# Top-1 routing moved into the attention stage, a fixed 448 places per expert, and expert weights in attention's buffers

## The chip, the cores and the metric

The kernel runs on one core of a Trainium2 chip: TensorE (PE, with its weight loads PEld), VectorE (DVE), ScalarE (ACT), GpSimd (POOL) and SyncE (SP), which run at their own pace and wait for one another by semaphores, and 16 DMA engines that move data between the chip's main memory and the on-chip buffers. The metric is the device time of one execution in microseconds, the median of several runs.

## What is computed

A gated linear attention, followed by a mixture of experts in which every token goes to one expert. The reference, cut to what matters:

```python
# 4 batches, 8 heads, 768 positions, 48 wide; complex state S
for t in range(S):
    S_re, S_im = a_re*S_re - a_im*S_im + k_t v_t^T, a_re*S_im + a_im*S_re
    y[t] = q_t @ S_re                       # a is first limited to |a| <= 0.999
x = y as 3072 rows of 384
logits = x @ w_gate                         # 8 experts
expert_idx = argmax(logits)
gate_w = softmax(logits)[expert_idx]
for e in range(8):
    mask = expert_idx == e
    h = max(x[mask] @ w1[e], 0)             # 384 -> 1024
    out[mask] = gate_w[mask] * (h @ w2[e])  # 1024 -> 384
```

All is fp32. How many tokens an expert gets depends on the data.

## The kernel before

**Attention** (lines 200 to 556) works batch by batch. Per batch, VectorE and ScalarE limit the gates (`limit`), run the recurrence over blocks of 16 positions (`front`, `fix`), and fold q and k with it (`fold`); SyncE's DMAs turn the folded tiles `pk` into one slot per head (`QX`, `KX`, a ring of six). Then `attention(b, g)` goes over the six chunks of 128 positions for a group of heads (three groups a batch): TensorE forms scores, VectorE masks them (`am`), TensorE forms outputs and the carried state (`st`, copied by ScalarE), ScalarE evicts rows to `xf`. In the last group of a batch each chunk's rows of `xf` are turned by TensorE, copied (`xt`) and multiplied by the routing weights `wgate` into logits; a SyncE DMA takes the rows to a table `x_hbm` in main memory, and the logits of a batch are copied to `lg_all`. None of this is emitted in the order of the source: each operation is registered with an engine, a cost, a delay and what it waits for, and a planner (`in_time`, lines 81 to 120) simulates them in turn, with priorities, and emits them in the order of their planned starts. The order on an engine is then fixed. In the profile they all carry line 132, where `InOrder` issues them.

**General path** (lines 559 to 637): `good` collects whether the numbers stayed in range. From it two trip counts are computed (`trips`, line 570), 0 or the whole count, of two loops: a slow exact recurrence and its logits. Every engine loads the counts and branches over the loops if they are 0.

**Routing** (lines 640 to 774), for all 3072 tokens at once: softmax gate, one-hot of the maximum, ranks within an expert by products with a triangular matrix (`rk`, lines 706 and 707), prefix sums, and an inversion by one-hot products (`A`, `J`, `ids`, line 757) which gives the lists `idx` (token of each place) and `widx` (weight rows of each tile). Experts are rounded up to whole tiles of 128 tokens; 31 tiles are always enough.

**Experts** (lines 777 to 815): 31 tiles in turn. GpSimd gathers the 128 token rows (`xs`, line 785) and the whole weights of the tile's expert (`w1t`, `w2t`, 3.1 MB, triple buffered); TensorE transposes the rows (`xt_ps`, line 797), multiplies 24 blocks of `w1t` (`h_ps`, line 804), ScalarE and VectorE apply the maximum with 0 (`ht`), TensorE multiplies by `w2t` (`o_ps`, line 810), VectorE multiplies by the gate (`yo`, line 812) and GpSimd scatters the rows to the output (line 813).

Of the kernel before, what the change touches and what calls it, by code (L numbers as in the profile page):

```python
# [33 lines left out]
W = DM + 1  # L34
LEAST = 1e-20
# [100 lines left out]
def gateloop_then_moe(ctx, tc, q, k, a_re, a_im, v, wg, w1, w2, out):  # L136
    nc = tc.nc
    x_hbm = nc.dram_tensor("x_hbm", (N + 1, W), FP32, kind="Internal").ap()

# [20 lines left out]
    with tc.tile_pool(name="zero", bufs=1) as setup:  # L160
        zrow = setup.tile([1, W], FP32, name="zrow")
        nc.vector.memset(zrow, 0.0)
        nc.sync.dma_start(x_hbm[N:N + 1, :], zrow)

# [30 lines left out]
    lg_all = route.tile([128, NT, E], FP32, name="lg_all")  # L195
    good = route.tile([128, B, G * C + 4], FP32, name="good")

    with ExitStack() as att:
# [13 lines left out]


# [9 lines left out]
        gates = [buf(f"gate{i}", JQ, 3, NC) for i in range(BL // JQ)]  # L223
        X = buf("X", BL, 2, NC)
        last, carry, zc = buf("last", 3, NC), buf("carry", 2, G * C, NB), [buf(f"zc{i}", 2, 2, G * C) for i in range(2)]
        lim = [[buf(f"{n}{i}", JQ, NC) for n in ("ls", "ll", "lu")] for i in range(2)]
        lsq, fsq = buf("lsq", JQ, 2, NC), buf("fsq", BL, 2, C * NB)
        fx = [buf(f"fx{i}", BL * C * (NB - 1)) for i in range(4)]
        zs = [buf(f"z{i}", 2, 2, NC) for i in range(2)]
# [4 lines left out]
        xf = buf("xf", C, DM)  # L234
# [6 lines left out]
        lg_ps = ps[7][:, 0:C * E].rearrange("p (c e) -> p c e", e=E)  # L241

        ops, used = [], {}
# [14 lines left out]
        def dma(late, emit, after=(), free=()):  # L258
            return op("S", 0.62, late, emit, after, free)

# [45 lines left out]
        def front(b, tiles):  # L306
# [5 lines left out]
            o = None  # L312
            for j in range(1, BL):
# [9 lines left out]
                state["z", w] = [o]  # L323
                state.setdefault(("gate", j // JQ), []).extend([m, c0] if j == 1 else [m])
# [19 lines left out]
            for t in tiles:  # L344
                state["carried", t] = [o, c0]
                state["X", t], state["carry", t] = [], []

# [74 lines left out]
        def attention(b, g):  # L422
# [24 lines left out]
            for c in range(C):  # L447
# [37 lines left out]
                def gather(c=c):  # L485
                    if own[0] == own[n - 1]:
                        A.activation(xf[:, c, hs[0] * D:hs[-1] * D + D].rearrange("p (h e) -> p h e", e=D), y_ps[:, 0:n, own[0]],
                                     func=ACT.Copy, scale=-1.0)
                    else:
                        for i, h in enumerate(hs):  # L490
                            A.activation(xf[:, c, h * D:h * D + D], y_ps[:, i, own[i]], func=ACT.Copy, scale=-1.0)
# [27 lines left out]
                if g == G - 1:  # L519
                    rows = state["row", b, c]  # L520

                    def across(c=c):
                        for d in range(DT):
                            T.transpose(px_ps[:, d, :], xf[:, c, d * 128:d * 128 + 128], ident)
# [9 lines left out]
                    r0 = b * S + c * 128  # L534
                    away = dma(5.0, lambda c=c, r0=r0: Q.dma_start(x_hbm[r0:r0 + 128, 0:DM].rearrange("(n j) w -> j n w", j=BL), xf[:, c, :]), rows)
                    state["xf", c] = [away, px]
            for i in slots:
                state["head", i] = [y]
            if g == G - 1:
                copy = act(C * E, lambda: A.copy(lg_all[:, b * C:(b + 1) * C, :], lg_ps), [lg], first=1)  # L540
                state["lg"] = [copy]
# [3 lines left out]
        for b in range(B):  # L545
            front(b, range(G))
            fixed = [fix(t) for t in range(G)]
            for t in range(G):
                fold(b, t, fixed[t])
                attention(b, t)  # L550
            if b + 1 < B:
                load_gates(b + 1)
                limit(b + 1)
        for o in in_time(ops):
            o.emit()


    with ExitStack() as fs:
        fp = fs.enter_context(tc.tile_pool(name="fp", bufs=1))
        fps = fs.enter_context(tc.tile_pool(name="fps", bufs=1, space=PSUM))  # L560
        nc.vector.tensor_scalar(out=good[:, :, G * C:], in0=good[:, :, G * C:], scalar1=MOST, scalar2=None, op0=ALU.is_le)
        least = fp.tile([128, 1], FP32, name="least")
        nc.vector.tensor_reduce(least, good.rearrange("p n c -> p (n c)"), axis=AX, op=ALU.min)
        ones_f = fp.tile([128, 1], FP32, name="ones_f")
        nc.vector.memset(ones_f, 1.0)
        n_good = fps.tile([1, 1], FP32, name="n_good")
        nc.tensor.matmul(n_good, lhsT=least, rhs=ones_f, start=True, stop=True)
        trips = fp.tile([1, 2], I32, name="trips")
        for u, n in enumerate((S // BL, NT)):
            nc.vector.tensor_scalar(out=trips[:, u:u + 1], in0=n_good, scalar1=127.5, scalar2=float(n),  # L570
                                    op0=ALU.is_lt, op1=ALU.mult)
        BG = B * G
        state = fp.tile([128, 2, BG, D], FP32, name="state")
        nc.gpsimd.memset(state, 0.0)  # L574

        own_i = fp.tile([128, G, H], I32, name="own_i")
        nc.gpsimd.iota(own_i, pattern=[[128, G], [-D, H]], base=0, channel_multiplier=1)
        own_f = fp.tile([128, G, H], FP32, name="own_f")
        nc.vector.tensor_copy(own_f, own_i)
        own = fp.tile([128, G, H], FP32, name="own")  # L580
        nc.vector.tensor_scalar(out=own, in0=own_f, scalar1=0.0, scalar2=None, op0=ALU.is_ge)
# [275 lines left out]
```

## Time and profile before

| | |
|---|---|
| time, median of 3 runs | 768.36 us (765.04 to 769.07) |
| profiled run | 768.0 us, span from first to last instruction 766.3 us |
| mean granted clock of TensorE | 0.946 |
| busy: PE, PEld, DVE, ACT, POOL | 79%, 68%, 51%, 37%, 18% |
| DMA | 156.50 MB, of which 108.36 MB on GpSimd's queue |

The page gives the busy time of each engine over the whole span and in 40 slices; a busy share over the span mixes the stages. The stretches give the same for chosen windows. The lines in order of time give the start, the length, the engine, source line and tiles of instructions or of runs of equal ones (x48), and in brackets how long the engine had been idle and what ended the idling. A record of a matrix product is one pass; an fp32 product makes two.

### The profile page before, as it was taken

Reading aid. Unit: us, or ns where it says so; the run is one execution under the profiler, and the core shown is the slowest. Engines: PE = TensorE matmul, PEld = TensorE weight load, DVE = VectorE, ACT = ScalarE, POOL = GpSimd, SP = SyncE. Lnnn points to the kernel's source line nnn. Section 1 sums busy time; section 2 is a strip of 40 time slices with the busy share of each in tenths; the row PEclk is TensorE's granted clock in tenths of the full one; section 3 lists DMA queues with packets and bytes.
Section 4 is the critical chain, followed back from the end, with each engine's and each line's share of the span. In section 5 each row is a group of like instructions: output and inputs, shape, how many; then the busy total and the mean of one; then the engine's idle time right before and its main releaser. Section 6 shows DMA issues by size and latency. Waiting matters only on the chain. (4 is left out here: it accounts for less than half of the span.)

```text
span 766.3 us, 11061 instructions
## 1 busy us (share of the span) xinstructions
PE 602.1 (79%) x3985; PEld 521.7 (68%) x3985; DVE 387.1 (51%) x720; ACT 280.3 (37%) x870; POOL 137.8 (18%) x160
## 2 busy tenths in 40 slices
PE   0000499789973999899317999999999999999997
PEld 0000499789963998899306787787787777787775
DVE  3999999989999999741261111111111111111111
ACT  4653799579985866775200000000000000000000
POOL 8000000000000000000112332342332442343221
PEclk9999999779985999999757999999999999999999
DMA  7131883486528706721019779789778988778930
GB/s 223 40 88 25 200 211 102 109 208 172 147 70 192 182 25 167 194 73 43 25 27 413 291 287 349 279 331 383 267 308 332 360 322 338 294 290 338 338 127 1
DMA packets 67630, 156.50 MB, mean 204 GB/s; under 512 B 9873, under 2 KB 50866, under 8 KB 59634
## 3 DMA queue, kind: packets, MB, share of 16 engines
q0 software_dynamic: 12896, 108.36, 36.9%
q1 hardware_dynamic: 51474, 47.36, 23.9%
q8 instruction: 33, 0.54, 0.3%
q10 hardware_dynamic: 3200, 0.01, 0.2%
q14 instruction: 27, 0.22, 0.1%
HBM read 127.23 MB, written 10.83 MB: 180 GB/s over the span
## 5 line engine op out<-in xcount | busy, mean ns | idle before, releaser
L804 PEld LDWEIGHTS h_ps<-xt,w1t 128*128 128x128 f32 x1488 | 172.9, 194 | 13.0 <-issue 5.0
L804 PE MATMUL h_ps<-xt,w1t 128*128 128x128 f32 x1488 | 173.2, 277 | 4.7 <-issue 4.7
L810 PE MATMUL o_ps<-w2t,ht 128*128 128x384 f32 x496 | 167.8, 492 | 8.5 <-ACT ht L806 8.2
L132 PE MATMUL bank<-QX,KX 128*128 128x224 f32 (+1 forms) x384 | 87.4, 367 | 102.6 <-DVE fl L132 86.1
L806 ACT ACTIVATE ht<-h_ps 128x512 f32<-128x512 f32 x31 | 18.5, 597 | 356.3 <-PE h_ps L804 356.3
L132 PEld LDWEIGHTS bank<-QX,KX 128*128 128x128 f32 x384 | 70.4, 207 | 105.0 <-issue 86.0
L810 PEld LDWEIGHTS o_ps<-w2t,ht 128*128 128x128 f32 x496 | 91.7, 190 | 71.7 <-ACT ht L806 14.2
L132 PE MATMUL bank<-st,QX 128*128 128x128 f32 x576 | 109.9, 279 | 1.7 <-ACT st L132 1.7
L812 DVE TENSOR_SCALAR yo<-o_ps,xs 128x384 f32<-128x384 f32 x31 | 19.2, 618 | 143.4 <-PE o_ps L810 143.4
L132 PEld LDWEIGHTS bank<-st,QX 128*128 128x128 f32 x576 | 87.9, 195 | 2.9 <-ACT st L132 2.9
L799 DVE COPY xt<-xt_ps 128x384 f32<-128x384 f32 x31 | 17.2, 556 | 139.4 <-PE xt_ps L797 139.4
L132 ACT ACTIVATE QX<-diag,KX 96x48 f32<-96x48 f32 x320 | 80.6, 329 | 3.8 <-DMA KX<-pk 3.7
L132 PE MATMUL bank<-vb,am 128*128 128x128 f32 x384 | 73.5, 282 | 4.9 <-DVE am L132 3.0
L813 POOL DMA_INDIRECT out_dram<-yo,idx x31 | 31.5, 1016 | 194.0 <-DVE yo L812 193.1
L132 PEld LDWEIGHTS bank<-vb,am 128*128 128x128 f32 x384 | 60.3, 196 | 6.6 <-DVE am L132 3.7
L574 POOL MEMSET state<- 128x1152 f32 x1 | 1.1, 1062 | 353.6 <-DMA x_hbm<-xf 353.6
L132 DVE TENSOR_TENSOR am<-bank,causal 128x256 f32<-128x256 f32 x120 | 43.0, 363 | 33.8 <-PE bank L132 28.9
L132 PE MATMUL bank<-vb,kt 128*128 128x128 f32 x320 | 59.4, 278 | 0.2 <-ACT kt L132 0.2
L132 PEld LDWEIGHTS bank<-vb,kt 128*128 128x128 f32 x320 | 48.2, 195 | 0.3 <-issue 0.3
L132 DVE TENSOR_TENSOR z<-gate,X 128x576 f32<-128x576 f32 x56 | 42.0, 750 | 0.6
L132 DVE TENSOR_TENSOR fx<-X,carry 128x672 f32<-128x672 f32 x48 | 38.5, 848 | 0.0
L785 POOL DMA_INDIRECT xs<-x_hbm,idx x31 | 30.2, 975 | 26.0 <-DVE idx L765 16.9
(143 smaller groups left out, 658.5 us busy)
## 6 DMA issues: line engine op xcount, KB each, us to landing
KX<-pk SPq DMA_DIRECT2D x48, 146.2 KB, 4.1
QX<-pk SPq DMA_DIRECT2D x48, 144.0 KB, 3.7
gate<-in_a_re_dram SPq DMA_DIRECT2D x16, 288.0 KB, 3.1
gate<-in_a_im_dram SPq DMA_DIRECT2D x16, 288.0 KB, 3.5
qt<-in_q_dram SPq DMA_DIRECT2D x12, 384.0 KB, 4.7
kt_in<-in_k_dram SPq DMA_DIRECT2D x12, 384.0 KB, 5.6
vb<-in_v_dram SPq DMA_DIRECT2D x24, 192.0 KB, 3.6
x_hbm<-xf SPq DMA_DIRECT2D x24, 192.0 KB, 2.9
```

The costliest lines, as they stand in the source:

```text
L132: return lambda *a, **kw: self.tc.keep_in_program_order(f(*a, **kw))
L574: nc.gpsimd.memset(state, 0.0)
L785: nc.gpsimd.indirect_dma_start(out=o, out_offset=None, in_=src, in_offset=bass.IndirectOffsetOnAxis(ap=index, axis=0))
L799: nc.vector.tensor_copy(xt, xt_ps)
L804: nc.tensor.matmul(h_ps[:, f, :], lhsT=w1t[:, c:c + 128], rhs=xt[:, d, :], start=(d == 0), stop=(d == DT - 1))
L806: nc.scalar.activation(ht[:, 0:FT // 2, :], h_ps[:, 0:FT // 2, :], func=ACT.Relu)
L810: nc.tensor.matmul(o_ps, lhsT=ht[:, f, :], rhs=w2t[:, f * DM:f * DM + DM], start=(f == 0), stop=(f == FT - 1))
L812: nc.vector.tensor_scalar_mul(y, o_ps, xs[:, DM:W])
L813: nc.gpsimd.indirect_dma_start(out=out[:, :], out_offset=bass.IndirectOffsetOnAxis(ap=idx[:, j:j + 1], axis=0), in_=y, in_offset=None, bou ...
```

## The change

Routing is done while attention runs, in five sends: one for each of the first three batches, and two for the last (chunks 0 to 3, chunks 4 and 5). A send computes the gate, the one-hot and the rank of each token within its expert, adds the next free row of the expert (`free_row`, carried from send to send), and scatters the rows from `xf` (now one buffer per chunk, 386 wide, with the gate and the token's number in the last two columns) straight to their place in a sorted table `sorted_x`. An expert has 448 places there that are used; they are filled beforehand with rows whose token number is out of range, so that their outputs are dropped. `x_hbm` is no longer written in attention.

The experts are then eight blocks of 448 places with plain loads of rows and weights: three tiles of 128 outputs and one half tile of 64. For the half tile the 384 output columns are split in two products of 192 that write to partitions 0 to 63 and 64 to 127 of one bank. Weights of three experts are held in `big[0..2]`; attention's gates, limits and squares, and X with its products, live in slices of the same buffers, and the first three fetches are planned on SyncE as soon as these are read for the last time.

The general path, now with the old routing and the old experts inside it, sits ahead of the experts in one loop of 0 or 1 trips. It runs if a number was out of range or an expert has more than 448 tokens; the experts then run after it on blank rows.

The diff, cut to its core:

```diff
+sends = [(b, 0, C) for b in range(B - 1)] + [(B - 1, 0, 4), (B - 1, 4, C)]
+big = [keep.tile([128, n], FP32, name=f"big{i}") for i, n in enumerate((12 * BL * NC // 4, 7296, 7296))]
+def fetch(e, queue):
+    for w, at, n in ((w1, 0, DT * F), (w2, DT * F, FT * DM)):
+        queue.dma_start(big[e % 3][:, at:at + n], w[e * 128:e * 128 + 128])
-gates = [buf(f"gate{i}", JQ, 3, NC) for i in range(BL // JQ)]
-X = buf("X", BL, 2, NC)
+gates = [part(0, JQ, 3, NC) for i in range(BL // JQ)]
+X = part(2, BL, 2, NC)
...
 lg = pe(3, logits, [turned_x], state.get("lg", []), first=rank)
-away = dma(5.0, lambda c=c, r0=r0: Q.dma_start(x_hbm[r0:r0 + 128, 0:DM].rearrange("(n j) w -> j n w", j=BL), xf[:, c, :]), rows)
-state["xf", c] = [away, px]
+for n_send, (sb, c0, c1) in enumerate(sends):
+    if (sb, c1 - 1) == (b, c):
+        send(n_send, b, c0, c1 - c0, lg)
...
+def send(k, b, c0, n, lg):
+    o = dve(wide, lambda: V.tensor_reduce(top, logit, axis=AX, op=ALU.max), [lg], free)
+    d = dve(wide, lambda: vtt(sub, logit, bc(top[:, :, None], full), ALU.subtract), [o])
...
+    T.matmul(rank, lhsT=before, rhs=oh, start=True, stop=(n == 1))
...
+    for i in range(n):
+        m = act(2, lambda i=i: A.copy(xfs[c0 + i][:, DM:WS], mark[:, i, :]), [gate, number], state.get(("xf", c0 + i), []))
+        move = pool_dma(4.0, away, [s, m, *state["blank"]] + state["row", b, c0 + i])
+        state["xf", c0 + i] = [move, state["x row", c0 + i]]
...
+for e in range(3):
+    op("S", 1.3, 20.0, lambda e=e: fetch(e, Q), (), wait)
...
+xs = load(0, room())
...
+stt(fine[:, 2:3], fine[:, 1:2], float(CAP), fine[:, 0:1], ALU.is_le, ALU.mult)
+n_gen = nc.values_load(trips[0:1, 0:1], min_val=0, max_val=1, ...)
+with tc.For_i(0, n_gen, 1):
+    general()
+    load(0, xs)
-for j in range(NTILE):
-    gather(xs, x_hbm[:, :], idx[:, j:j + 1])
-    gather(w1t, w1[:, :], widx[:, j:j + 1])
-    gather(w2t, w2[:, :], widx[:, j:j + 1])
...
+xt = turned(xs)
+for e in range(E):
+    if e + 1 < E:
+        xs_next = load(e + 1, room())
+    w1t, w2t = weights(e)
+    for f in range(FT):
+        for d in range(DT):
+            T.matmul(h, lhsT=w1t[:, d, f * 128:f * 128 + 128], rhs=xt[:, d, :], start=(d == 0), stop=(d == DT - 1))
...
+    if e + 1 < E:
+        xt = turned(xs_next)
+    for i in range(TT):
+        for f in range(FT):
+            T.matmul(o, lhsT=ht[:, f, i * 128:i * 128 + 128], rhs=w2t[:, f, :], start=(f == 0), stop=(f == FT - 1))
...
+    for f in range(FT):
+        for u in range(2):
+            T.matmul(o[u * 64:u * 64 + 64, 0:HALF], lhsT=ht[:, f, TT * 128:CAP], rhs=w2t[:, f, u * HALF:u * HALF + HALF],
+                     start=(f == 0), stop=(f == FT - 1))
...
+    if e + 3 < E:
+        fetch(e + 3, nc.sync)
```

## Prediction

> **What bounds the kernel now.** I read the page's busy shares over the span first, then the stretches of the span, then the lines in order of time around the joint between the two halves, then one expert tile near the end. The page:
>
> ```profile
> span 766.3 us, 11061 instructions
> ...
> PE 602.1 (79%) x3985; PEld 521.7 (68%) x3985; DVE 387.1 (51%) x720; ACT 280.3 (37%) x870; POOL 137.8 (18%) x160
> ...
> PE   0000499789973999899317999999999999999997
> ...
> PEclk9999999779985999999757999999999999999999
> ```
>
> No engine is at 100%, so there are stages with different limits. The stretches (columns: length, then busy us of PE, PEld, DVE, ACT, POOL, then clock, DMA share, GB/s):
>
> ```profile
> 20.00:80.00 60.00, 0.00 (x0) 0.00 (x0) 59.38 (x96) 31.54 (x53) 0.00 (x0) 1.00 0.23 63
> ...
> 240.00:330.00 90.00, 83.22 (x609) 80.12 (x610) 81.97 (x150) 68.36 (x256) 0.00 (x0) 0.94 0.57 143
> ...
> 330.00:360.00 30.00, 30.00 (x242) 29.86 (x241) 8.56 (x20) 19.11 (x80) 0.00 (x0) 1.00 0.21 53
> ...
> 371.30:406.70 35.40, 2.94 (x31) 2.19 (x32) 16.82 (x63) 1.84 (x3) 9.02 (x15) 0.53 0.24 70
> ...
> 406.70:750.00 343.30, 334.48 (x2011) 264.65 (x2012) 52.69 (x89) 17.91 (x30) 111.42 (x115) 0.99 0.81 310
> ```
>
> Attention (to 371.3 us) is VectorE's until about 330 and TensorE's from there. 371 to 407 is a hole in which TensorE works 2.9 of 35.4 us. From 407 TensorE works 97%. In order of time, the joint:
>
> ```profile
> 370.45 0.83 PE L132 MATMUL bank<-wgate,xt 128*128 128x8 f32 x6 [0.57 <-ACT xt L132]
> ...
> 373.55 0.21 DVE L570 TENSOR_SCALAR trips<-n_good 1x1 int32<-1x1 f32 x2 [0.33 <-PE n_good L567]
> ...
> 379.89 0.35 DVE L683 TENSOR_REDUCE mx<-lg_all 128x24 f32<-128x192 f32 x1 [5.27 <-SPq L637]
> ...
> 397.76 1.13 POOL L785 DMA_INDIRECT xs<-x_hbm,idx  x1 [16.91 <-DVE idx L765]
> ...
> 399.19 0.95 POOL L785 DMA_INDIRECT w1t<-in_moe_w_dram,widx  x1 [0.30 <-issue]
> ...
> 406.71 7.54 PE L804 MATMUL h_ps<-xt,w1t 128*128 128x128 f32 x48 [4.65 <-issue]
> ```
>
> The last logits end at 371.3, the two skipped loops cost 373.8 to 379.8, routing on VectorE 379.9 to 397.5, the first rows and weights 397.8 to 406.7. Then one tile of the experts:
>
> ```profile
> 738.52 5.52 PE L804 MATMUL h_ps<-xt,w1t 128*128 128x128 f32 x48
> ...
> 743.88 0.49 PE L797 MATMUL xt_ps<-ident,xs 128*128 128x128 f32 x3
> ...
> 744.73 5.43 PE L810 MATMUL o_ps<-w2t,ht 128*128 128x384 f32 x16 [0.36 <-ACT ht L806]
> ...
> 749.99 5.52 PE L804 MATMUL h_ps<-xt,w1t 128*128 128x128 f32 x48
> ...
> 756.20 5.43 PE L810 MATMUL o_ps<-w2t,ht 128*128 128x384 f32 x16 [0.69 <-ACT ht L806]
> ```
>
> A tile starts every 11.47 us (738.52 to 749.99), 31 tiles. Each fp32 product is two passes: 48 records of 128 columns in 5.36 us are 0.112 us each, 16 of 384 in 5.26 us are 0.329 us each. That is a line of 0.003 us plus 0.00085 us per column.
>
> **What the Trainium skill says.** "TensorE: Matmul & The Clock Gate", Part 1, lets the clock fall to half in an idle window of some 3.4 us; the trace agrees: 0.53 in the hole, and the first 48 passes took 7.54 us instead of 5.36. The same page's Part 3 (Packing small matmuls) says that products with few output rows run side by side in different column groups, three of 32 rows 2.38 times as fast as in turn; nothing in this trace shows that. "Runtime: NRT & Kernel Launch", Instruction fetch mechanics, says that a taken branch far ahead costs a fetch; the trace agrees in kind (5.8 us for two skipped loops). "DMA: Bandwidth & Descriptors", Issuing engines are not separate DMA queues, says that all queues share the same 16 engines; so early writes of blanks and weights compete with attention's loads.
>
> **The change, part by part.**
> *Attention.* Five sends are added, each about 12 VectorE operations of 16 to 48 columns. The nearest row, 128x36, takes 0.22 us each; in a stream of independent operations starts are about 0.1 us apart. So a send costs 1.2 to 2.6 us, and three sends (first three batches) lie in VectorE's own stretch: 3.6 to 8; I take 5. ScalarE's copies of gate and number (24 of some 0.2 us) hide: it has 20% free. The 4+4 small products of the fourth send lie in TensorE's stretch: 1 us. The setups, the memory shared with weights and the dropped x_hbm writes I cost at nothing: VectorE works 8.2 of the first 20 us, and the built order shows no new waits between the slices of a shared buffer. The eight blank fills (5.5 MB) land in 20 to 60 us, where DMA is at 0.2 busy and VectorE sets the pace. Row buffers are now held until a whole batch is sent: after the last logits of batch 0 (about 160) the sends need some 10 us, and the first row of batch 1 was evicted at 165. TensorE can stand 5 us there, hidden as it has 16 of 80 us free. The weights of experts 0 to 2 go in SyncE's queue ahead of the last batch's value loads and last QX and KX loads; SyncE waits there for gates, fsq and X to be read. 3.1 MB at the 310 GB/s seen are 10 us. The second lot follows the fs at 320.6 and ends near 333, when the last KX loads are issued anyway (332.5), so nothing on the path. Last logits: 371.3 + 6 = 377.3.
>
> *The joint.* The 35.4 us go, and this chain comes: 6 small operations to the one-hot (1.3), ranks (0.5, as the two rk products), 3 operations (0.7), handing to GpSimd 0.3, two scatters 1.25 apart, the last landing 2.9 after its start: 6.9, so 384.2. Then two things in parallel, both waiting for those scatters: rows of expert 0 (three issues of 0.5, landing about 3 later, 388.7), and the check (1.3) plus one skipped loop. One of two loops would be 2.9 us of 5.8, all of it 5.8; the body jumped over is larger now, I take 4: 389.5. Every engine waits at this branch, TensorE's transposes queue behind it. Twelve transposes at half clock and the last copy 3.5: first expert product at 393.0, against 406.7.
>
> *The experts.* h: 24 products of 448 columns, 48 passes of 0.383: 18.4. Transposes of the next rows: 12 of about 0.11, with a stall for the third buffer: 1.6. Three output tiles: 48 passes of 0.329: 15.8. The half tile: 32 passes of 192 columns on 64 output rows, 0.166 each. In turn 5.3; perfectly side by side 2.7; with the skill's 2.38 of 3 as yield, 1.6 times, an estimate of 3.3. Sum 39.1. Evictions hide (128x512 takes 0.60 and one h group 2.3). Weights are read 8 times, not 31: 3.1 MB plus 0.6 MB of rows take 12 us at the speed seen, while h alone takes 18.4: hidden, although the rows queue behind the weights. Eight times 39.1 less the 1.6 counted in the joint is 311.2; cold clock again 2.2. TensorE ends at 706.4. From the end of the last product to the end of the span it was 761.6 to 766.3, 4.7: 711.1. The time before is 2.1 over its span: 713.
>
> **Rivals.**
> *Half tiles in turn (0.22).* For: two passes of one product share a column group, so neighbours can't always pair. Against: the built program places them in two different column groups. 8 times 2.0 more: 729; with weight loads in the open (190 ns) up to 738.
> *Attention grows (0.13).* The row buffers and the weights ahead of loads in one queue delay TensorE where it has no slack (last batch, 100% busy), or VectorE suffers at each batch border: some 20 us beyond my 6, 733. For: the last KX loads are issued from 332.5, land in 4.5 us each, and are used from 339.6. Against: TensorE's idle gaps of up to 14 us at batch borders.
> *The general path runs (0.03).* An expert with over 448 tokens sends the kernel through the old way and back: at least the old 355 us more, over 1,060: slower. Against: the reference's inputs give 338 to 421 tokens per expert.
>
> **How the numbers follow.** The first case has 0.62, spread 702 to 722 by the branch (2.9 to 5.8), the sends (3.6 to 8) and the half tile (2.7 to 5.3). Below 701 I leave 0.05 (full pairing and hidden sends); above 735 the tails of the second and third case and the fourth, 0.12. So 713, 701 to 735. All but the last case are over 0.5% faster: faster 0.96, same 0.01, slower 0.03.
>
> **What would show it.** Last logits at 377; the first expert product at 393; expert period 39 us, h passes 0.383; half tile 3.3 or 5.3 us; DMA in the experts near 90 GB/s; no instruction of the general path. Wrong if TensorE waits for KX or xf in the last batch, if the branch costs over 6, or if h waits for weights.

## The result, and the profile after

The changed kernel takes 742.86 us (median of 4 runs, 739.98 to 744.19) against 768.72 us for the kernel before on the same chip: ratio 0.966, 95% interval 0.960 to 0.971. It is faster by 25.9 us, where 55 were forecast. The page of the profile after, the lines that answer to those of before:

```profile
span 742.5 us, 9030 instructions
...
PE 575.0 (77%) x3050; PEld 424.0 (57%) x3050; DVE 367.9 (50%) x714; ACT 296.9 (40%) x924; POOL 84.7 (11%) x101
...
PE   0000059985399979988898399999999999999995
...
PEclk9999999996689989998999599999999999999999
```

A slice is 18.6 us. TensorE begins in the sixth slice, where before it began in the fifth; the hole ahead of the experts, three slices before (3, 1, 7), is one slice now (the last 3), but lies at 408 us; behind it stand nines up to the last slice. The stretches (length, busy us of PE, PEld, DVE, ACT, POOL, then clock, DMA share, GB/s):

```profile
20.00:80.00 60.00, 0.00 (x0) 0.00 (x0) 46.77 (x79) 25.21 (x41) 4.17 (x6) 1.00 0.60 142
...
240.00:330.00 90.00, 82.03 (x624) 77.75 (x622) 87.01 (x165) 63.44 (x226) 6.84 (x6) 0.94 0.63 168
330.00:360.00 30.00, 23.34 (x146) 19.97 (x147) 20.80 (x42) 20.26 (x87) 6.17 (x6) 0.89 0.88 261
...
405.10:424.20 19.10, 3.81 (x19) 2.30 (x17) 3.25 (x21) 2.32 (x5) 3.73 (x4) 0.59 0.38 122
424.20:734.10 309.90, 309.25 (x1109) 173.30 (x1108) 38.55 (x76) 30.41 (x55) 30.11 (x31) 0.99 0.24 83
```

VectorE, which had 59.38 busy us between 20 and 80, has 46.77, while the DMA share went from 0.23 to 0.60. TensorE, 30.00 of 30 us busy between 330 and 360 before, has 23.34. The joint is 19.1 us instead of 35.4, the experts 309.9 instead of 354.9. In order of time around the joint:

```profile
404.29 0.83 PE L134 MATMUL bank<-wgate,xt 128*128 128x8 f32 x6 [0.57 <-ACT xt L134]
...
409.11 0.97 POOL L645 DMA_INDIRECT sorted_x<-xf,slot  x1 [0.30 <-issue]
412.45 0.38 SPq L688 DMA_DIRECT2D xs<-sorted_x  x1
...
412.91 0.17 DVE L150 TENSOR_TENSOR fit<-free_row 128x8 f32<-128x8 f32 x1 [5.83 <-DMA sorted_x<-xf,slot]
...
414.03 0.15 DVE L735 TENSOR_SCALAR trips<-n_fine 1x1 int32<-1x1 f32 x1 [0.54 <-PE n_fine L734]
...
420.84 3.45 PE L134 MATMUL xt_ps<-ident,xs 128*128 128x128 f32 x12 [6.85 <-issue]
...
424.22 1.11 PE L134 MATMUL h_ps<-xt,big 128*128 128x448 f32 x1
```

The last logits end at 405.1 (before 371.3, forecast 377.3). The last scatter starts at 409.11 and has landed when the row load is issued at 412.45. The trip count is there at 414.18; TensorE and VectorE then stand until 420.8 behind the skipped loop (ScalarE has its first instruction behind it at 417.96). Of these 6.7 us TensorE's own branch instruction takes 3.40 (415.79 to 419.19); in the kernel before none of its branches took over 0.33. One expert:

```profile
620.12 18.31 PE L134 MATMUL h_ps<-xt,big 128*128 128x448 f32 x48
638.27 2.23 PE L134 MATMUL xt_ps<-ident,xs 128*128 128x128 f32 x12
640.43 18.50 PE L134 MATMUL o_ps<-big,ht 128*128 128x384 f32 x80
658.86 18.31 PE L134 MATMUL h_ps<-xt,big 128*128 128x448 f32 x48
```

From start to start: h 18.15 us, transposes 2.16, outputs 18.43, period 38.74. Of the outputs 48 passes of 0.329 are 15.8, so the 32 passes of the half tile took 2.6.

Where the forecast span (711.1) and the measured one (742.5) part:

| stage | forecast | measured | difference |
|---|---|---|---|
| last logits | 377.3 | 405.1 | +27.8 |
| joint, to the first expert product | 15.7 | 19.1 | +3.4 |
| experts | 313.4 | 309.9 | -3.5 |
| last product to end of span | 4.7 | 8.4 | +3.7 |

So the miss is attention. There the delay can be added up on VectorE: the start of its first scan operation, the end of its last fold operation (`pk<-big,fl` of batch 3), and the sum of its idle times in brackets, from the bracket of that first operation on. Before: 9.6, 333.2, idle 19.4. After: 11.7, 360.5, idle 39.6. The last fold is 27.3 us later: 2.1 for a later start, 20.2 for stalls, and the rest, 5.0, is added work, as forecast. From the last fold to the last logits it took 38.1 us, now 44.6: 6.5 more. Together 33.8 us over the kernel before, of which 6 were forecast.

The largest stall, with what leads to it. The first line is from the page's DMA issues (KB each, median us from issue to landing), the second and third are SyncE's gate loads of batch 1, the last two lines of ScalarE and VectorE:

```profile
sorted_x<-empty POOLq DMA_DIRECT2D x8, 675.5 KB, 16.0
```

```profile
18.33 5.83 POOL L664 DMA_DIRECT2D sorted_x<-empty  x8 [0.32 <-POOL empty L281]
...
29.99 2.35 SPq L134 DMA_DIRECT2D big<-in_a_im_dram  x1
...
40.13 4.49 SPq L134 DMA_DIRECT2D big<-in_a_im_dram  x1
...
51.05 1.74 ACT L134 ACTIVATE big<-big 128x1152 f32<-128x1152 f32 x2 [14.68 <-DMA big<-in_a_im_dram]
52.25 0.76 DVE L134 SCALAR_TENSOR_TENSOR big<-big 128x576 f32<-128x576 f32 x1 [12.61 <-ACT big L134]
```

All eight blank fills are issued in a row at 18.33, as soon as their source `empty` is filled. The planner had spread them over eight scan and fix operations, but that is a matter of its model only: nothing on the chip makes a fill wait for those. The fills land one after another, the first at 25.66 and the last at 49.88. The two gate loads issued at 29.56 and 29.99 land 18.7 and 21.0 us after their issue, at 48.29 and 50.97, where the same two landed after 2.9 and 3.3 us before. SyncE's issue of a gate load takes 2.35 and 4.49 us where it took 0.51 and 0.45 before, ScalarE waits 14.68 us for a gate, and VectorE 12.61 us for ScalarE.

The second place is the border of the first two batches. GpSimd's scatters of batch 0, ScalarE's and TensorE's next work:

```profile
193.76 5.45 POOL L645 DMA_INDIRECT sorted_x<-xf,slot  x1 [169.59 <-DVE big L134]
199.52 3.02 POOL L645 DMA_INDIRECT sorted_x<-xf,slot  x1 [0.30 <-issue]
```

```profile
201.06 0.25 ACT L134 ACTIVATE xf<-bank 128x96 f32<-128x96 f32 x1 [2.98 <-DMA sorted_x<-xf,slot]
```

```profile
201.36 0.79 PE L134 MATMUL bank<-vb,am 128*128 128x128 f32 x2 [9.66 <-ACT xf L134]
```

The last logits of batch 0 end at 168.1; the send's VectorE operations lie at 180.1 to 192.9 behind folds in the queue, the first scatter starts at 193.76, and until it has landed the first row of batch 1 can't be evicted.

The third is the last batch: SyncE issues weights at 346.56, and the QX loads behind them take from 348.37 on:

```profile
346.56 1.32 SPq L134 DMA_DIRECT2D big<-in_moe_w_dram  x2
348.37 11.41 SPq L134 DMA_DIRECT2D QX<-pk  x3
```

The QX load issued at 348.37 landed 13.4 us later, and the last KX loads were issued only from 359.89 on.

### The profile page after: what moved, and what is told of

Its sections match the earlier page's. It is cut to its first block, busy times and chain, and to the rows that moved or that the text cites. A ratio compares the mean times of both kernels' runs of the same rounds, so it can differ in the third digit from the quotient of the medians.

```text
span 742.5 us, 9030 instructions
## 1 busy us (share of the span) xinstructions
PE 575.0 (77%) x3050; PEld 424.0 (57%) x3050; DVE 367.9 (50%) x714; ACT 296.9 (40%) x924; POOL 84.7 (11%) x101
## 5 line engine op out<-in xcount | busy, mean ns | idle before, releaser
L134 PE MATMUL h_ps<-xt,big 128*128 128x448 f32 x384 | 148.8, 548 | 0.0
L134 PE MATMUL o_ps<-big,ht 128*128 128x384 f32 (+1 forms) x640 | 147.9, 424 | 0.0
L134 PEld LDWEIGHTS bank<-QX,KX 128*128 128x128 f32 x384 | 69.5, 209 | 125.1 <-issue 101.9
L134 PEld LDWEIGHTS o_ps<-big,ht 128*128 128x128 f32 (+1 forms) x640 | 90.1, 169 | 56.1 <-issue 4.7
L134 PEld LDWEIGHTS h_ps<-xt,big 128*128 128x128 f32 x384 | 73.3, 193 | 71.8 <-issue 71.2
L134 ACT ACTIVATE big<-big 128x576 f32<-128x576 f32 (+2 forms) x92 | 79.3, 872 | 46.3 <-DVE big L134 26.4
L134 PE MATMUL bank<-vb,am 128*128 128x128 f32 x384 | 75.9, 289 | 16.5 <-ACT xf L134 15.7
L645 POOL DMA_INDIRECT sorted_x<-xf,slot x24 | 31.2, 1301 | 354.7 <-DVE big L134 169.6
L1020 ACT ACTIVATE ht<-h_ps 128x448 f32<-128x448 f32 x32 | 17.4, 543 | 132.6 <-PE h_ps L134 132.6
L134 DVE TENSOR_TENSOR big<-big,big 128x576 f32<-128x576 f32 (+1 forms) x72 | 62.8, 883 | 0.6
L134 DVE TENSOR_TENSOR big<-big 128x288 f32<-128x288 f32 (+2 forms) x104 | 60.7, 599 | 1.1 <-ACT big L134 0.6
L134 DVE TENSOR_TENSOR am<-bank,causal 128x256 f32<-128x256 f32 (+1 forms) x120 | 42.3, 363 | 34.2 <-PE bank L134 30.6
L710 POOL DMA_INDIRECT out_dram<-yo,to x24 | 23.3, 972 | 282.0 <-ACT yo L1031 248.5
```

Of the source, the lines that this page charges most:

```text
L134: return lambda *a, **kw: self.tc.keep_in_program_order(f(*a, **kw))
L645: move = nc.gpsimd.indirect_dma_start(out=sorted_x[:, :], out_offset=bass.IndirectOffsetOnAxis(ap=slot[:, i:i + 1], axis=0), in_=xfs[c0 + ...
L710: move = nc.gpsimd.indirect_dma_start(out=rows, out_offset=bass.IndirectOffsetOnAxis(ap=index, axis=0), in_=y, in_offset=None, bounds_chec ...
L1020: nc.scalar.activation(ht[:, f, :], h, func=ACT.Relu)
```

## The experiments

All are edits of the changed kernel, except before_fills, which is one of the kernel before. Times are medians; ratios are to the kernel before on the same chip, with 95% intervals. Where two intervals overlap, the times alone don't tell the two kernels apart. The other columns come from one profiled execution each: in five of them whose attention is the same (changed, check_early, no_general, half_in_turn, tail_one) the last logits end between 400.8 and 405.1, so a shift of some 4 us there is no effect by itself.

| run | us | ratio | first score | last logits | first expert product |
|---|---|---|---|---|---|
| before | 768.7 | 1 | 86.1 | 371.3 | 406.7 (+35.4) |
| changed | 742.86 | 0.966 (0.960 to 0.971) | 101.9 | 405.1 | 424.2 (+19.1) |
| blanks_wait | 735.85 | 0.959 (0.955 to 0.964) | 89.7 | 396.9 | 416.3 (+19.4) |
| before_fills | 786.86 | 1.025 (1.022 to 1.027) | 101.5 | 387.0 | 423.1 (+36.1) |
| blank_small_wait | 729.45 | 0.949 (0.945 to 0.953) | 88.4 | 393.7 | 412.8 (+19.2) |
| weights_late | 739.61 | 0.962 (0.960 to 0.965) | 102.0 | 400.0 | 419.1 (+19.1) |
| sends_first | 741.00 | 0.964 (0.961 to 0.967) | 101.2 | 402.9 | 422.0 (+19.1) |
| sends_split | 741.92 | 0.963 (0.961 to 0.965) | 101.5 | 404.8 | 423.6 (+18.8) |
| check_early | 741.50 | 0.965 (0.962 to 0.968) | 101.4 | 404.9 | 422.4 (+17.5) |
| no_general | 736.43 | 0.960 (0.956 to 0.963) | 101.4 | 400.8 | 415.7 (+14.9) |
| half_in_turn | 764.43 | 0.994 (0.992 to 0.996) | 101.4 | 404.9 | 424.1 (+19.2) |
| best1 | 725.94 | 0.945 (0.942 to 0.947) | 87.5 | 386.6 | 404.6 (+18.0) |
| best2 | 723.69 | 0.941 (0.939 to 0.942) | 88.2 | 386.7 | 404.0 (+17.3) |
| best3 | 721.94 | 0.938 (0.936 to 0.940) | 87.3 | 384.1 | 402.2 (+18.1) |
| best4 | 730.09 | 0.944 (0.940 to 0.949) | 88.1 | 392.9 | 411.5 (+18.6) |
| best5 | 727.97 | 0.942 (0.938 to 0.946) | 87.6 | 390.9 | 409.8 (+18.9) |
| best6 | 722.86 | 0.939 (0.934 to 0.943) | 88.2 | 384.5 | 401.9 (+17.4) |
| best7 | 721.53 | 0.937 (0.933 to 0.941) | 87.0 | 384.5 | 402.1 (+17.6) |

The kernel before took 772.8 us beside best4 and best5 and 768.5 to 769.4 beside the others, so those two are compared by ratio. best3 was run again beside best6 and best7: 722.73, 0.938 (0.934 to 0.941).

**blanks_wait: each fill waits on the chip for what it was planned behind.**

```diff
-state["blank"] = [pool_dma(10.0, lambda e=e: nc.gpsimd.dma_start(sorted_x[...], bc(empty[:, None, :], ...)), [o]) ...]
+def blank(e, at):
+    P.tensor_copy(tick[:, e:e + 1], at)     # one element of that operation's result
+    P.dma_start(sorted_x[...], bc(empty[:, None, :], ...))
```

> Edit: each of the eight blank fills now waits on the chip for the scan or fix operation of batch 0 behind which it was planned (GpSimd first copies one element of that operation's result). Theory (the fills, issued all at once at 18 to 24 us, starve the gate loads of batch 1): VectorE's wait of 12.6 us at 52 us is gone or under 3 us, the first score product comes at 86 to 91 us instead of 101.9, and the time falls from 742.9 by 8 to 16, to 727 to 735. Rival (VectorE waits for something else there, as the shared buffers): first score product still at 99 to 102, time 743. Second rival (attention catches up later, or the row buffers take it back): first scores early, but time within 3 of 743.

VectorE's wait of 12.6 us at 52 is gone (it works without a gap there), the first score comes 12.2 us sooner, the median falls by 7.0 (the intervals still touch). The burst is the cause of the late start; but five of the 12 us don't arrive at the end. GpSimd's lines say why the fills still hurt:

```profile
72.24 7.92 POOL L134 COPY tick<-big 1x1 f32<-1x1 f32 x1
80.10 0.70 POOL L134 DMA_DIRECT2D sorted_x<-empty  x1
80.80 10.98 POOL L134 COPY tick<-big 1x1 f32<-1x1 f32 x1
91.73 0.70 POOL L134 DMA_DIRECT2D sorted_x<-empty  x1
92.43 0.17 POOL L134 COPY tick<-big 1x1 f32<-1x1 f32 x1
```

Copies of one element take 8 and 11 us (their recorded time) beside VectorE's folds, so the last three fills come at 80 to 93, among the first QX, KX, q and k loads (DMA 0.96 busy from 80 to 100), and VectorE then waits for q:

```profile
104.15 1.83 DVE L134 TENSOR_TENSOR pk<-big,qt 128x768 f32<-128x768 f32 x2 [3.52 <-DMA qt<-in_q_dram]
```

**before_fills: the fills alone, in the kernel before.**

```diff
+for e in range(E):
+    nc.gpsimd.dma_start(sorted_x[e * N:e * N + CAP]..., bc(empty[:, None, :], ...))   # at the start, as in the changed kernel
```

> Edit: the kernel before, with only the eight blank fills of the changed kernel added at its start, all issued at once (nothing reads them). Theory (the burst starves the gate loads of batch 1): VectorE waits some 12 us at about 50 us, first score near 99 instead of 86, time 8 to 13 over the kernel before, 776 to 782. Rival (the wait in the changed kernel comes of the shared buffers or of the planner's order): first score at 86 to 88, time 769 to 770.

```profile
52.66 0.76 DVE L134 SCALAR_TENSOR_TENSOR ls<-lsq 128x576 f32<-128x576 f32 x1 [15.73 <-ACT lsq L134]
```

The same stall, without sends, shared buffers or another order, and 18.4 us more on the whole kernel (786.86 against 768.51 on the same chip), more than expected: the full stall of 15.7 arrives at the end of attention (last logits 15.7 later), and from the last product to the end of the span it takes 6.4 us instead of 4.7. So the fills alone make the stall; it needs neither the shared buffers nor the planner's order.

**blank_small_wait: fewer bytes.** As blanks_wait, with places 320 to 447 only, and a check ahead of the experts that each has at least 320 tokens; with fewer the general path runs. So this kernel, and every best kernel below, keeps the fast way for fewer inputs than the changed one.

```diff
+LOW = 320
-P.dma_start(sorted_x[e * N:e * N + CAP]...
+P.dma_start(sorted_x[e * N + LOW:e * N + CAP]...
+nc.vector.tensor_reduce(fine[:, 1:2], fit, axis=AX, op=ALU.min)
+stt(fine[:, 2:3], fine[:, 1:2], float(LOW), fine[:, 2:3], ALU.is_ge, ALU.mult)
```

> Edit: as blanks_wait, and each fill covers only places 320 to 447 of its expert (1.58 MB in all instead of 5.5); the check ahead of the experts then also asks that each expert has at least 320 tokens. Theory (what blanks_wait did not give back is DMA time of the late fills, which meet the loads of QX, KX and k at 80 to 100 us, DMA 0.96 busy): first score at 87 to 89, VectorE's wait for q at 104 gone, last fold of the last batch 2 to 4 us sooner than in blanks_wait (352.3), time 731 to 734. Rival (the rest is row buffers and order): last fold at 352, time 736.

729.45, a little better than expected. The first score is at 88.4, the wait for q at 100 is two of 0.30, the last fold ends at 349.4 (352.3 in blanks_wait). So late and smaller fills give back 13.4 of the 742.9 us, clear of noise: by far the largest term. Time and size change together here; blanks_wait changes the time alone. Whether the bytes of the fills or their many rows of 1544 bytes weigh more was not tested.

**weights_late: the weights behind all loads of attention.**

```diff
-op("S", 1.3, 20.0, lambda e=e: fetch(e, Q), (), wait)
 for o in in_time(ops):
     o.emit()
+for e in range(3):
+    fetch(e, Q)
```

> Edit: the weights of experts 0 to 2 are fetched by SyncE after the last load of attention instead of ahead of the last batch's last loads. Theory (the 3.1 MB each lie ahead of QX, KX and v in the DMA engines): from the last logits of batch 2 (333.2) to those of batch 3 (405.1) it takes 66 us or less instead of 71.9, and the time falls by 5 to 8, to 735 to 738; the first expert does not wait for its weights. Rival (this stage is slow by the held rows and by VectorE, which runs late): 71 to 72 us as before, time 743, or later if the first expert now waits for its weights.

```profile
330.00:360.00 30.00, 26.94 (x181) 24.36 (x182) 21.63 (x44) 22.76 (x96) 6.28 (x6) 0.89 0.70 173
```

From the last logits of batch 2 (333.5) to those of batch 3 (400.0) it takes 66.5 us instead of 71.9; in the stretch 330 to 360 TensorE works 26.94 us instead of 23.34. The QX load that took 13.4 us to land takes 2.8. The first expert does not wait for its weights. The stage's 66.5 lies below the 68.7 to 73.2 of the five profiles with unedited attention. The median falls by 3.3, less than was expected, and the intervals overlap: the weights' delay is shown in the trace, its size in the whole time is not clear of noise.

**sends_first and sends_split: held rows.** The first gives a send's VectorE and ScalarE operations the planner's highest priority, the second sends every batch in two parts.

```diff
-sends = [(b, 0, C) for b in range(B - 1)] + [(B - 1, 0, 4), (B - 1, 4, C)]
+sends = [(b, *cs) for b in range(B) for cs in ((0, 4), (4, C))]      # sends_split
```

> Edit: the VectorE and ScalarE operations of a send get the planner's highest priority, nothing else. Theory (sends come late, so rows of xf are held, and TensorE stands): in the first send the last VectorE operation follows the last logits within 6 us (25 in the changed kernel: 168.1 to 192.9), TensorE's waits for ScalarE's xf at 200 to 210 fall from 9.7 and more to under 3 in all, and the time falls by 5 to 12, to 731 to 738. Rival (VectorE sets the pace up to 330 us, and it does the same work in another order): time within 3 of 743.

> Edit: the changed kernel with every batch sent in two parts (chunks 0 to 3, then 4 and 5), nothing else. Theory (held rows): TensorE's waits for xf in the second batch fall from 11 to under 3, VectorE's stall of 4.2 us at 208 goes, time 737 to 740. Rival (VectorE's added work weighs more): 743 to 748.

Neither alone does anything that the runs can tell from the changed kernel (intervals overlap). In sends_first the waits for xf in the second batch go, as the theory said, though the first send is done only 10.9 us after the last logits (165.6 to 176.5) and not within 6. But a new wait stands in their place:

```profile
173.31 0.20 PE L134 MATMUL bank<-oh,before 128*128 128x48 bf16 x1 [7.73 <-DVE oh L134]
```

TensorE's rank product was put ahead in its order and waits 7.7 us for a one-hot that goes back and forth between VectorE and ScalarE; and VectorE does the same folds, only in another order. sends_split keeps 11.2 us of xf waits in the second batch, so its theory falls too, and TensorE waits 10.8 us for KX at 176.6, where the changed kernel has a wait of 7.8 for QX at 175.9.

**best1 to best5: together.** best1 is blank_small_wait, weights_late and check_early (below).

> Edit: blank_small_wait, weights_late and check_early together. Theory (three separate causes, so their gains add): 742.9 less 13.4 less 3.3 less 1.4, that is 724 to 727; the first score at 88, last fold 346, last logits 386 to 389. Rival (they overlap, one wait takes the place of another): 729 or more.

> Edit: best1, and every batch sends its rows in two parts (chunks 0 to 3, then 4 and 5), not the last batch alone. Theory (rows of xf are held until a whole batch is sent, which stalls TensorE, ScalarE and through it VectorE for some 4 us at 196 to 210): TensorE's waits for xf in the second batch fall from 11 to under 3, VectorE's 4.4 us stall goes, time 3 to 6 below best1. Rival (three more sends of 12 small VectorE operations in the stretch where VectorE sets the pace, 2 us each): 0 to 5 above best1.

> Edit: best2 with the VectorE and ScalarE operations of a send at the planner's highest priority. Theory (the send's operations lie behind folds in VectorE's order, so that even four rows are held long): time 2 to 5 below best2. Rival (an in-order engine at the front of its queue waits for the step on another engine before, and TensorE's ranks stall as in sends_first, 7.7 us for the one-hot): above best2 by up to 5.

> Edit: best1 with the VectorE and ScalarE operations of a send at the planner's highest priority, batches sent whole. Theory (what holds the rows is the lateness of the send's operations, and the three added sends of best3 cost VectorE 2.7 us for nothing): last fold 341 to 344, time 718 to 721. Rival (the whole send lands too late for the first rows, and TensorE stalls at the one-hot): 723 to 727.

> Edit: best4, with the rank and count products of a send behind the next batch's products in TensorE's priority. Theory (the rank products, placed at the head of TensorE's order, make it wait for the one-hot, up to 7.7 us in sends_first): TensorE's wait for the one-hot is under 2 us, time 2 to 5 below best4. Rival (the ranks now come later and the rows are held longer): as best4 or up to 4 above.

best1 gives 725.94, inside the theory's range: the gains of its three parts, 13.4, 3.3 and 1.4, add up to within 1.1 us, as separate causes would, though the two small ones are within noise taken alone. Sending in halves (best2) brings 2.3 us more, its interval just touching best1's, but not as the theory said: TensorE's wait for xf in the second batch is still 9.8 us. Halves and early together (best3) bring 4.0 us, to 0.938, with an interval clear of best1's, and that wait is gone. Early alone, with whole batches (best4), brings nothing against best1 (0.944 against 0.945), and has the 7.7 us at the one-hot again; in best5 that wait is still 7.2, so its theory falls. Placing the rank products later (best5, and best7 against best6) moves the ratio by 0.003 and 0.002, within the intervals. So what could be won from held rows and late sends is 4.0 us, net of the work of three more sends; their cost without that work was not measured. Not all of attention's delay is repaired: best3's last logits end at 384.1, still 6.8 us after the forecast. Added up on VectorE as above, best3 has start 11.4, last fold 346.3, idle 22.7, against 9.6, 333.2 and 19.4 before: 1.7 for the start, 3.3 for stalls, and 8.0 for added work, six sends ahead of the last fold. Its stretches:

```profile
20.00:80.00 60.00, 0.00 (x0) 0.00 (x0) 59.35 (x96) 30.51 (x49) 23.57 (x12) 1.00 0.29 75
...
330.00:360.00 30.00, 29.36 (x231) 28.19 (x230) 13.42 (x30) 24.72 (x101) 1.94 (x2) 1.00 0.78 243
```

VectorE is busy throughout 20 to 80 again (59.35, before 59.38), TensorE in 29.36 of the 30 us to 360.

**check_early, no_general, best6: the branch.** check_early gives `fit`, `fine`, `ones_f` and `trips` memory of their own, so that the check does not wait for the scatters that read memory it got from attention.

```diff
+cp = ctx.enter_context(tc.tile_pool(name="cp", bufs=1))     # ahead of attention's pools
+fit, fine = cp.tile([128, E], FP32, name="fit"), cp.tile([128, 3], FP32, name="fine")
...
-    cp = cs.enter_context(tc.tile_pool(name="cp", bufs=1))
```

> Edit: the tiles of the range check (fit, fine, ones_f, trips) get memory of their own instead of memory that the row buffers of attention held. Theory (the check waits 5.8 us at 407 to 413 only because its memory is read by the last scatters; behind them stand check, trip count and branch): fit starts right after the last slots, the branch ends while the scatters land, the first expert product comes 3 to 5 us sooner after the last logits (19.1 us now), time 738 to 740. Rival (the branch is ordered behind the row loads of expert 0, which wait for the scatters anyway): 18.5 to 19.1 us, time 743.

> Edit: the changed kernel without its general path: the trip count is computed but not loaded, and no loop stands ahead of the experts (left out: the way for numbers out of range or an expert with over 448 tokens). Theory (the branch itself is on the path, 6.65 us from trip count to the end of the skipped loop): the first expert product comes 12 to 15 us after the last logits instead of 19.1, time 736 to 739. Rival (the rows of expert 0, issued after the scatters land, come in only 1 to 2 us before the branch ends): 17 to 18 us, time 741. The end: if the 8.4 us from the last product to the end of the span belong to the code of the general path, they fall to about 5.

In check_early the trip count is ready at 407.6, 6.6 us sooner, and the joint is 17.5 instead of 19.1: less than the theory said. The trip count no longer holds, but all engines wait for SyncE at the branch, and SyncE stands behind row loads that wait for the scatters: it issues the last of them until 415.8, and TensorE goes on at 419.0. The time, 741.50, is not told apart from the changed kernel's. Without the branch (no_general) the joint is 14.9, and the rows end the wait:

```profile
409.63 0.15 DVE L735 TENSOR_SCALAR trips<-n_fine 1x1 int32<-1x1 f32 x1 [0.54 <-PE n_fine L734]
...
412.38 3.42 PE L134 MATMUL xt_ps<-ident,xs 128*128 128x128 f32 x12 [2.79 <-DMA xs<-sorted_x]
```

So the branch costs 4.2 us of the joint beyond what the rows take anyway. (In its profile attention also ended 4.3 us sooner, where nothing was edited; that part of its 6.4 us is not explained.) best6 puts the row loads behind the loop:

```diff
-xs = load(0, room())
+xs = room()
 ...
 with tc.For_i(0, n_gen, 1):
     general()
-    load(0, xs)
+load(0, xs)
```

> Edit: best3 with the row loads of expert 0 issued after the loop of the general path instead of ahead of it. Theory (in best3 all engines wait at the branch for SyncE, which stands in its queue behind row loads that wait for the scatters): the branch is over before the scatters have landed, the first expert product comes 14 to 15.5 us after the last logits instead of 18.1, as in no_general (14.9), and the time falls by 3 to 4 us. Rival (the engines reach the loop's end at the same time anyway, since it is the skipped code's fetch that takes long, and the rows are now issued after it): 18 us or more, no gain.

> Edit: best6 with the rank and count products of a send behind the next batch's products in TensorE's priority. Theory (rank products at the head of TensorE's order stall it for VectorE's small operations, 4.9 us in best3's first batch): that wait goes and the time falls by 1 to 4. Rival (the ranks come later, rows are held longer): equal or up to 4 above best6.

> The kernel of best3 again, beside the next two. Both theories: ratio to the kernel before 0.936 to 0.940, first expert product 18 us after the last logits.

```profile
387.46 0.15 DVE L747 TENSOR_SCALAR trips<-n_fine 1x1 int32<-1x1 f32 x1 [0.37 <-PE n_fine L746]
...
394.25 0.40 SPq L704 DMA_DIRECT2D xs<-sorted_x  x1
...
398.54 3.45 PE L135 MATMUL xt_ps<-ident,xs 128*128 128x128 f32 x12 [11.12 <-DMA xs<-sorted_x]
```

The theory falls. From trip count to the first instruction behind the loop it is 6.6 us here (387.61 to 394.25), as in the changed kernel (414.18 to 420.84, 6.7). TensorE's branch instruction alone takes 3.82 of them here. Where SyncE comes late, as in check_early and best3, TensorE's branch (3.96 and 3.80) is over before SyncE arrives, and the engines leave some 3 to 4 us after SyncE's last row load. With the row loads behind the loop, their 4.3 us are paid after the branch instead of before, and nothing is gained. Why TensorE's branch takes so long was not tested.

**half_in_turn: one product of 384 columns for the half tile.**

```diff
-for u in range(2):
-    T.matmul(o[u * 64:u * 64 + 64, 0:HALF], lhsT=ht[:, f, TT * 128:CAP], rhs=w2t[:, f, u * HALF:u * HALF + HALF], ...)
+T.matmul(o[0:64, :], lhsT=ht[:, f, TT * 128:CAP], rhs=w2t[:, f, :], ...)
```

> Edit: the half tile of an expert is one product of 384 columns on 64 output rows instead of two of 192 that write to partitions 0 to 63 and 64 to 127. Theory (the two halves run side by side): 16 passes of 0.329 us take 5.3 us instead of the 2.64 that the 32 passes of 192 columns take now, 2.6 us more per expert, the expert period 41.4 instead of 38.74, time 763 to 765. Rival (nothing runs side by side, a pass with 64 weight columns is simply that fast): period 38.7, time 743.

```profile
653.07 21.05 PE L134 MATMUL o_ps<-big,ht 128*128 128x384 f32 x64
674.05 11.17 PE L134 MATMUL h_ps<-xt,big 128*128 128x448 f32 x29
```

The outputs take 20.98 us from start to start instead of 18.43, the experts 330.4 instead of 309.9, the time 764.43, as the theory said. 16 passes of 384 columns take 5.2 us, the 32 of 192 columns in the changed kernel 2.6; in its trace the two passes of a pair start 7 ns apart.

**tail_one: the end.** The three scatters of the last expert's whole tiles are left out, so these output rows are not written. It is a single profiled run.

```diff
-    to_out(y, out, to[:, i:i + 1])
+    if e + 1 < E:
+        to_out(y, out, to[:, i:i + 1])
```

> Edit: the changed kernel without the scatters of the last expert's three whole output tiles (left out: these rows of the output); its half tile is still scattered. Theory (GpSimd's last drain has to see several scatters off): from the last product to the end of the span 4.5 to 6 us instead of 8.4. Rival (a fixed cost of ending this program): 8 to 8.5 us.

7.6 us instead of 8.4: neither the theory's 4.5 to 6 nor quite the rival's 8 to 8.5. The longest step of the end is a drain, an instruction with which GpSimd waits at the end of the program. The profile's lines of GpSimd's drains (durations in ns: shortest, median, longest), for the changed kernel, tail_one and the kernel before:

```profile
L1083 POOLq DRAIN  x3: 40/246/6516, 734.6 to 742.2; - x3
```

```profile
L1084 POOLq DRAIN  x3: 40/109/6276, 733.3 to 740.1; - x3
```

```profile
L853 POOLq DRAIN  x3: 45/109/3088, 762.3 to 766.0; - x3
```

The drain takes 6.52 us where it took 3.09: 3.4 of the 3.7 us. It stays at 6.46 with whole rows in the half tile (half_in_turn), at 6.51 without the general path (no_general), and at 6.28 without the three scatters, so none of these is its cause. In before_fills, which adds only the fills to the kernel before, it takes 4.91: 1.8 us come with the fills. Why, and where the rest comes from, stays open.

## Why the prediction was wrong, point by point

- **"The eight blank fills (5.5 MB) land in 20 to 60 us, where DMA is at 0.2 busy and VectorE sets the pace": the step that failed.** They did land in that stretch, but the conclusion, that they cost nothing, was wrong: late and smaller fills give 13.4 us back (blank_small_wait), and the fills alone cost the kernel before 18.4 (before_fills). The share of 0.2 was a mean over 60 us. The fills all issue at 18.3, and the gate loads of batch 1, without which ScalarE and so VectorE can't go on, stand in exactly that stretch and land up to 21.0 us after their issue instead of 3.3. The prediction itself said that all queues share the same 16 engines, and that early writes compete with attention's loads; it did not ask which load was due next. It also took the spread that the planner's code shows for a spread on the chip, though no instruction waits for it. Of the 29.9 us between forecast and result this step is 13.4; the rest is made of the smaller terms below.
- **The weights "ahead of the last batch's ... loads ... so nothing on the path": failed.** The stage got 5.4 us shorter without them (weights_late); of the time it is 3.3, within noise. The second lot followed the last fs as forecast, but that came at 346.2 and not 320.6, since attention ran late; the last QX loads then stood behind it and landed after 13.4 us, and the last KX loads after those.
- **Rows held, "TensorE can stand 5 us there, hidden": failed, but small.** The last logits of batch 0 did not end at "about 160" in the kernel before: the sixth chunk's products end at 173.9, after the first row of batch 1 is evicted (165.3). And a send was thought to need 10 us after them; in the changed kernel the first scatter started 25.7 us after, and TensorE waited 9.66 us for xf. Won back were 4.0 us net (best1 to best3).
- **The setups, costed at nothing:** VectorE's first scan operation starts 2.1 us later (11.7 for 9.6). No run took this apart.
- **VectorE's 5 us for three sends: right**, 5.0 as the rest of the sum above.
- **The joint:** scatters landed 7.3 after the last logits (412.45 is when the row load follows; forecast 6.9), check 1.27 (1.3), transposes 3.4 (3.5): right. The branch, 4 us forecast from a range of 2.9 to 5.8, took 6.7: only its size was off, and the condition named in the forecast, "if the branch costs over 6", came true. The estimate went by the number of loops; the larger part of the 6.7 is TensorE's one branch instruction.
- **The experts: right, slightly too dear.** Period 38.74 for 39.1; h 18.15 for 18.4; the half tile 2.6 for 3.3, but the transposes 2.16 for 1.6, so in part errors cancel; no wait for weights, 83 GB/s for "near 90". That the sum came out 3.5 too high hid as much of the other misses: luck.
- **The end**, 8.4 for 4.7: it was taken over from the kernel before; off by the drain.
- **The rival "Attention grows"** was the one that came, with 27.8 us beyond the forecast instead of 20, but for its largest part not by what it named: row buffers and weights together won back some 7 us, the fills 13.4. "Half tiles in turn" was wrong: half_in_turn shows what it would have cost (21.6 us), and the changed kernel does not pay it.
- **Slips of the working, all small:** the two skipped loops take 6.0 us by the lines shown (373.8 to 379.8), not 5.8; the profiled time is 1.7 over its span (768.0 and 766.3), not 2.1; and the three terms named for the first case span 706 to 734, not 702 to 722.

## What to carry to other kernels

A low mean DMA share is no room for a burst: look up which load is due in the stretch, and what engine waits for it, before a background transfer is called hidden. An order that a planner gives to DMAs binds only what the hardware waits for, so look in the trace for the start of the first one. Repairs of separate causes can add up: here fills, weights and check did to within 1.1 us, and with earlier sends in halves (best3) they give 721.9 us, 0.938 of the kernel before, where the change as made gives 0.966; the price is the general path for any expert with under 320 tokens.

## What the runs showed of the hardware that was not expected

- Two products of 192 columns with 64 output rows each, written to partitions 0 to 63 and 64 to 127, ran side by side without loss: 32 passes in 2.6 us, against 5.2 for 16 passes of 384 columns. The Trainium skill, "TensorE: Matmul & The Clock Gate", Part 3 (Packing small matmuls), tells of 2.38 for three tiles of 32 rows; here two tiles of 64 gave 2.0 of 2. The forecast had taken the same yield for both.
- GpSimd's copy of one element took 0.17 us at best and 10.98 beside VectorE's unbroken run of operations with two inputs (blanks_wait), and the first two scatters of batch 0 took 5.45 and 3.02 us where later ones took 0.97. The Trainium skill, "SBUF — State Buffer", SBUF: two separate sides, says that GpSimd and VectorE share a pair of ports by an exclusive lock, and that a VectorE operation with two SBUF inputs takes it too, against a GpSimd operation that reads SBUF. The copies agree: those that start at 66.90, 72.24 and 80.80 end within 0.15 us of the start of the next VectorE operation without two SBUF inputs (71.47, 80.03 and 91.67), so they outlast whole runs of operations and not one. That the scatters are slow for the same reason is argued, not shown. A GpSimd instruction is therefore a poor clock for timing a transfer in a stretch that VectorE fills.
- A skipped loop with a large body took 6.7 us from trip count to TensorE's first instruction behind it (changed kernel) and 6.6 to SyncE's (best6); two loops with smaller bodies took some 6 together in the kernel before. TensorE's branch instruction took 3.40 to 3.96 us of it (changed kernel, check_early, best3, best6), and at most 0.33 in the kernel before.
- GpSimd's last drain took 3.09 us in the kernel before, 4.91 with the eight fills added (before_fills) and 6.52 in the changed kernel.
